# Loads behind marker stores in the start-up of a decay-attention and softplus-FFN kernel

## The chip, the core and the metric

The kernel runs on one core of a Trainium2 chip. A core has a matrix engine (TensorE, PE in the profile; its weight loads are PEld), a vector engine (VectorE, DVE), a scalar engine (ScalarE, ACT), a general engine (GpSimd, POOL) and a synchronising engine (SyncE, SP) that here issues nearly all DMA transfers. Each engine has its own instruction stream and runs it in order; semaphores tie the streams together. The metric is device time in microseconds of one execution, lower is better.

## The reference

Attention with a decaying state, for 4 batches, 8 heads, 768 positions and 64 dimensions, in blocks of 64 positions, and then a feed-forward layer on the 3072 tokens of 512 values:

```python
for b in range(nb):                       # 12 blocks of 64 positions
    intra = np.einsum('bhic,bhjc->bhij', qb, kb) * Dmask[None]
    intra = np.einsum('bhij,bhjd->bhid', intra, vb)
    inter = np.einsum('bhid,bhde->bhie', qb * lam_pow[None], kv_state)
    out[:, :, sl] = intra + inter
    kb_dec = kb * rev_pow[None]
    kv_state = lam_block[None, :, None, None] * kv_state + np.einsum('bhsd,bhse->bhde', kb_dec, vb)
...
h = x @ w_in                              # 512 -> 2048
g = np.maximum(h, 0.0) + np.log1p(np.exp(-np.abs(h)))
return (g @ w_out).astype(np.float32)     # 2048 -> 512
```

`q`, `k`, `v` and the decay `lam` are float32; the two weight matrices are float64 as drawn.

## The kernel before

The 768 positions are cut into six chunks of 128 (two blocks each). The attention of one chunk and one pair of heads is a *unit*: 24 units in all, four per chunk. Unit `g` is loaded by `load_upto` (L84) in two DMA transfers of 512 KB. The weights come in 32 *banks* of 512 KB, half of them of the first matrix, half of the second, loaded by `w_load` (L126) as raw 64-bit words into tiles `raw`. A bank is converted on the chip: `w_scale` and `w_round` on ScalarE (L213, L217), `w_shift`, `w_sign` and `w_add` on VectorE (L221, L225, L231), then split into a high and a low part, `w_hi` on ScalarE (L234) and `w_lo` on VectorE (L238). Both layers' matmuls run as three products of such parts.

A unit has these steps. `k_decay` (L281 for unit 0, L285 otherwise, on ScalarE) and `q_decay` (L292) scale keys and queries. `mm_scores` (L307, L309; `xy` in the order list) forms scores and state updates on TensorE; in the first chunk one matmul at L301 opens it. `mask_scores` (L334) multiplies by the decay mask; `first_states` (L347) and `next_states` (L359) copy states on ScalarE, `carry_states` (L354) carries them on TensorE. `mm_out` (L322, L326; `z`) forms the unit's output, and `x_high` (L371, ScalarE) and `x_low` (L378, VectorE) split it into parts for the feed-forward layer.

The feed-forward layer runs in 96 *slots*: 6 chunks times 16 slices of 128 of the 2048 hidden values. `mlp1` (L406) makes a slot's hidden values from four units' outputs, `chain_act` (L387, softplus), `chain_hi` (L391) and `chain_lo` (L395) make its parts `g`, and `mlp2` (L423) adds them into four output banks, one per batch. At a chunk's last slot each bank is copied out by ScalarE or VectorE (L429) and stored (L431).

Eight DMA semaphores are used in turn, so SP issues a transfer only when the one eight places earlier has landed. Work goes to the engines in the order in which the code is written: a list of named steps for the first chunk's attention and the first slots (`for line in """ ... """`), and a loop over slots after it. In the list, `load n` loads weight banks up to n, `unit n` units up to n, and `warm n` issues n filler matmuls (L146) into a bank that nobody reads. `act`, `ghi` and `glo` are a slot's `chain_*` steps. Ahead of the list, units 0 to 3 and weight banks are loaded in turn, 18 fillers run, and the decay tables are built.

Of the kernel before, what the change touches and what calls it, by code (L numbers as in the profile page):

```python
# [7 lines left out]
F32 = mybir.dt.float32  # L8
# [6 lines left out]
B, H, S, D = 4, 8, 768, 64  # L15
C = 128
T = 64
NCH = S // C
NP = H // 2
# [7 lines left out]
def half(i):  # L27
    return slice(i * 64, (i + 1) * 64)
# [3 lines left out]
def decay_attention_softplus_ffn(  # L32
# [7 lines left out]
    nc = tc.nc  # L40
    ctx.enter_context(tc.manual_schedule())
    cp = ctx.enter_context(tc.tile_pool(name="cp", bufs=1))
# [5 lines left out]
    def t8(shape, dt, name):  # L48
        return sb.tile(shape, dt, tag="b8", bufs=21, name=name)
# [4 lines left out]
    def t2(shape, dt, name):  # L54
        return sb.tile(shape, dt, tag="b2", bufs=5, name=name)
# [7 lines left out]
    def obank(name):  # L63
        return ps.tile([128, 512], F32, tag="o", bufs=4, name=name)
# [5 lines left out]
    def bank(name):  # L70
        return ps.tile([128, 512], F32, tag="h", bufs=2, name=name)
# [8 lines left out]
    def load_upto(n):  # L80
        for g in range(len(units), min(n, NG)):
            t = t8([128, 2, 2, 512], F32, f"att{g}")
            for major in range(2):
                nc.sync.dma_start(out=t[:, major], in_=att[g // NP, g % NP, :, major])  # L84
            units.append(t)
# [33 lines left out]
    def w_load(n):  # L119
        nonlocal n_raw  # L120
        while n_raw < min(n, NW):
            k = n_raw
            if k % 2 == 0:
                raws[k] = raws[k + 1] = t8([128, 2, DM, 2], U32, f"raw{k}")
            f, which = w_order[k]
            nc.sync.dma_start(  # L126
                out=raws[k][:, k % 2].rearrange("q n t -> q (n t)"), in_=wts[f, which].bitcast(U32)
            )
            n_raw += 1

    for n in range(NP - 1):
        load_upto(n + 1)
        w_load(n + 1)
    load_upto(NP)
    w_load(7)
    load_upto(NP + 1)


    spare = t8([128, 4, 512], F32, "spare")
    warm = t8([128, 512], F32R, "warm")  # L140
# [12 lines left out]
    for s in range(2):  # L153
# [7 lines left out]
        out=begins[0], in_=ramp.rearrange("q (o i) -> q o i", o=1).broadcast_to([128, H, T]), scalar=0.0,  # L161
# [9 lines left out]
    def powers(out, n):  # L171
# [19 lines left out]
        out=diag[half(1)], in0=off[half(1)].rearrange("q (o i) -> q o i", o=1).broadcast_to([64, H, T]), scalar=0.0,  # L191
# [48 lines left out]
    def w_of(f, which):  # L240
        j, i = divmod(w_order.index((f, which)), 2)
        return w_pairs[j][:, :, i]
# [7 lines left out]
    def x_of(c, p):  # L250
        if (c, p // 2) not in x_tiles:
            x_tiles[c, p // 2] = t8([128, 2, 2, 512], F32R, f"x_{c}_{p // 2}")
        return x_tiles[c, p // 2][:, :, p % 2]

    aa, kds, qds, states = {}, {}, {}, {}
    lo, hi = half(0), half(1)
# [5 lines left out]
    def first_chunk(g):  # L262
        return g < NP
# [6 lines left out]
    def own(g, n, name):  # L270
        if not first_chunk(g):
            return t2([128, B, 2, 64], F32, f"{name}_{g}")
        if g not in spares:
            spares[g] = t8([128, 3, B, 2, 64], F32, f"own_{g}")
        return spares[g][:, n]
# [107 lines left out]
    h_tiles, l_tiles, g_tiles, o_tiles = {}, {}, {}, {}  # L383
# [13 lines left out]
    def mlp1(s, ps_=range(NP)):  # L397
        c, f = divmod(s, NF)
        if s not in h_tiles:
            h_tiles[s] = bank(f"h{s}")  # L400
        w = w_of(f, 0)
        for p in ps_:
            cs = slice(p * 128, (p + 1) * 128)
            x = x_of(c, p)
            for n, (i, j) in enumerate(((0, 0), (1, 0), (0, 1))):
                nc.tensor.matmul(  # L406
                    h_tiles[s], lhsT=w[:, i, cs], rhs=x[:, j, :],
                    start=p == 0 and n == 0, stop=p == NP - 1 and n == 2,
                )

    def mlp2(ss):
        c = ss[0] // NF
        ends = ss[-1] % NF == NF - 1
        if ss[0] % NF == 0:
            o_tiles[c] = [obank(f"o{c}_{b}") for b in range(B)]
        if ends:
            ob = t8([128, B, 512], F32, f"ob{c}")
        for b in range(B):
            for s in ss:
                f = s % NF  # L420
                g, w = g_tiles[s], w_of(f, 1)
                for n, (i, j) in enumerate(((0, 0), (0, 1), (1, 0))):
                    nc.tensor.matmul(  # L423
                        o_tiles[c][b], lhsT=g[:, i, b * 128 : (b + 1) * 128], rhs=w[:, j],
                        start=f == 0 and n == 0, stop=f == NF - 1 and n == 2,
                    )
            if ends:
                copy = nc.vector.tensor_copy if b % 2 else nc.scalar.copy
                copy(out=ob[:, b], in_=o_tiles[c][b])  # L429
                queue = nc.scalar if c == NCH - 1 and b % 2 == 0 else nc.sync  # L430
                queue.dma_start(out=out[b * S + c * C : b * S + (c + 1) * C, :], in_=ob[:, b])  # L431
# [11 lines left out]
    xy, z = {}, {}  # L443
# [5 lines left out]
    def end(p):  # L449
# [6 lines left out]
        "dg": lambda p: carry_states(p, xy[p][1]), "sl": lambda p: next_states(p, xy[p][1]), "xh": lambda p: x_high(p, z[p]),  # L456
        "xl": lambda p: x_low(p, z[p]), "scale": w_scale, "round": w_round, "shift": w_shift, "sign": w_sign,
        "add": w_add, "hi": w_hi, "lo": w_lo, "act": chain_act, "ghi": chain_hi, "glo": chain_lo,
        "mlp": lambda s, *ps_: mlp1(s, ps_ or range(NP)), "scores": scores_of, "load": w_load, "unit": load_upto, "warm": keep_warm,
    }  # L460
    for line in """
        q 0, k 0, xy 0, scale 0, round 0, a 0, st 0, q 1, warm 3, shift 0, sign 0, z 0, add 0, k 1, xh 0,
        xl 0, hi 0, xy 1, dg 0, scale 1, lo 0, st 1, a 1, q 2, round 1, mlp 0 0, warm 4, sl 0, shift 1,
        sign 1, z 1, add 1, k 2, xy 2, dg 1, xh 1, xl 1, hi 1, scale 2, round 2, lo 1, a 2, st 2, sl 1, q
        3, mlp 0 1, warm 4, load 8, shift 2, sign 2, add 2, k 3, z 2, xy 3, xh 2, xl 2, hi 2, scale 3,
        round 3, shift 3, a 3, st 3, lo 2, sign 3, dg 2, mlp 0 2, warm 2, add 3, z 3, mlp 1 0, mlp 1 1,
        mlp 1 2, scale 4, round 4, xh 3, hi 3, sl 2, xl 3, shift 4, lo 3, sign 4, add 4, load 10, mlp 0 3,
        mlp 1 3, scale 5, round 5, q 4, k 4, act 0, ghi 0, hi 4, shift 5, sign 5, add 5, lo 4, dg 3, mlp
        2, act 1, ghi 1, hi 5, glo 0, glo 1, lo 5, scale 6 7, round 6 7, scores 4, unit 6, load 12, act 2,
        ghi 2, mlp 3, glo 2, sl 3, shift 6 7, sign 6 7, add 6 7  # L470
    """.replace("\n", " ").split(","):
        name, *numbers = line.split()
        step[name](*map(int, numbers))
# [11 lines left out]
    for s in range(LAG, last + LAG):  # L485
# [19 lines left out]
        if s == last + LAG - 2:  # L505
            mlp2([s - LAG, s - LAG + 1])
        elif s - LAG < last - 1 and s - 1 not in both_at:
            mlp2([s - LAG])
# [4 lines left out]
        if s in both_at:  # L513

            g = both_at[s]
            w, x, y = work(f"z{g - 1}"), bank(f"x{g}"), bank(f"y{g}")
            mm_out(g - 1, w)
            mm_scores(g, x, y)
            mask_scores(g, x)
            x_high(g - 1, w)  # L520
            update_states(g, y)
            x_low(g - 1, w)
            if g < NG - 1:
                keep_values(g)
            mlp2([s + 1 - LAG])
# [51 lines left out]
```

## Time and profile before

| | |
|---|---|
| Time, three runs | 607.14, 607.69 (median), 608.19 us |
| The profiled execution | 607.95 us |
| Its span, first to last instruction of the program | 606.2 us |
| TensorE busy | 596.9 us, 98% of the span |
| VectorE, ScalarE busy | 226.4 us, 219.8 us |
| HBM read, written | 41.95 MB, 6.29 MB |

The span is shorter than the time by 1.75 us, which lies outside the program's instructions. A matmul's end is modelled, and matmuls overlap, so a busy TensorE is not one at its peak. In a row of a timeline stand the start, the length in us, the engine, the line of the code, the operation, the tiles written and read, their shapes and the number of instructions merged; in brackets stands the idle time of the engine before it and what ended it. "issue" there means that nothing which the profile records ended the wait. In rows of grouped waits stand the total in us, how often, and the longest. A row of stretches has the stretch, its length, for each engine the busy time and the number of instructions, then TensorE's granted clock (1.00 is full), the mean busy share of the 16 DMA engines, and GB/s.

### The profile page before, as it was taken

How to read it: one execution, taken by the hardware profiler on the slowest of the kernel's cores; microseconds unless marked ns; L12 is line 12 of the kernel's file. 1: busy time of each engine (PE TensorE's matmuls, PEld its weight loads, DVE VectorE, ACT ScalarE, POOL GpSimd, SP SyncE). 2: the span in 40 equal slices, each digit the busy share in tenths (PEclk: the TensorE clock that was granted, in tenths of full speed). 3: DMA queues.
4: the chain of work that ended last, by engine and by line, in shares of the span. 5: the costliest groups of instructions: out<-in, count | busy, mean ns of one | idle time of the engine just before them, and what ended most of it. 6: DMA issues, size and time to landing. Idle time of an engine off the chain costs nothing.

```text
span 606.2 us, 11776 instructions
## 1 busy us (share of the span) xinstructions
PE 596.9 (98%) x5299; PEld 488.5 (81%) x5299; DVE 226.4 (37%) x336; ACT 219.8 (36%) x355; POOL 4.7 (1%) x11
## 2 busy tenths in 40 slices
PE   9899999999999999999999999999999999999997
PEld 6577888888888888888888888888888888888886
DVE  7779999853232233132222321321312211211111
ACT  3777777633222223332223323222333121322121
POOL 3000000000000000000000000000000000000000
PEclk9999999999999999999999999999999999999999
DMA  8995314216002023300120500211500000100001
GB/s 297 406 406 227 122 74 141 88 52 208 3 2 70 1 70 98 112 2 11 61 70 29 182 2 0 71 32 40 207 3 1 1 1 1 69 2 0 1 0 69
DMA packets 15169, 48.98 MB, mean 81 GB/s; under 512 B 1808, under 2 KB 1808, under 8 KB 15120
## 3 DMA queue, kind: packets, MB, share of 16 engines
q1 hardware_dynamic: 14832, 47.72, 21.8%
q8 instruction: 41, 0.67, 0.4%
q10 hardware_dynamic: 288, 0.52, 0.2%
q14 instruction: 8, 0.07, 0.0%
HBM read 41.95 MB, written 6.29 MB: 80 GB/s over the span
## 4 chain that ended last, share of the span: by engine, by line
PE 91%; DMA 7%; DVE 1%; SPq 1%; ACT 0%; issue 0%
PE o L423 43%; PE h L406 41%; DMA raw<-in_wts 5%; PE z L322 2%; PE x L307 2%; DMA att<-in_att 2%; PE z L326 2%; PE w L307 1%; PE y L309 1%; SPq L84 0%; DVE w L238 0%; DVE c L231 0%; DVE c L225 0%; SPq L126 0%; ACT w L234 0%; PE w L309 0%
## 5 line engine op out<-in xcount | busy, mean ns | idle before, releaser
L423 PE MATMUL o<-w,g 128*128 128x512 f32 x1152 | 278.9, 391 | 1.1 <-DVE w L238 0.8
L406 PE MATMUL h<-x,w 128*128 128x512 f32 x1152 | 276.8, 391 | 0.0
L423 PEld LDWEIGHTS o<-w,g 128*128 128x128 f32 x1152 | 215.0, 188 | 47.2 <-DVE w L238 1.1
L406 PEld LDWEIGHTS h<-x,w 128*128 128x128 f32 x1152 | 215.1, 188 | 46.7 <-issue 1.2
L395 DVE TENSOR_TENSOR g<-l,g 128x512 fp32r<-128x512 f32 x96 | 66.4, 692 | 310.4 <-ACT g L391 310.2
L387 ACT ACTIVATE l<-h 128x512 f32<-128x512 f32 x96 | 57.4, 598 | 309.0 <-PE h L406 306.4
L391 ACT CAST g<-l 128x512 fp32r<-128x512 f32 x96 | 59.6, 621 | 3.1
L371 ACT CAST x<-z 128x512 fp32r<-128x512 f32 x24 | 14.0, 585 | 41.4 <-PE z L326 41.4
L334 DVE TENSOR_TENSOR a<-x,mask 128x512 f32<-128x512 f32 x15 | 10.4, 692 | 36.1 <-PE y L309 26.4
L339 DVE SCALAR_TENSOR_TENSOR st<-st,lam_c,y 64x256 f32<-64x256 f32 x52 | 22.9, 480 | 0.8
L322 PEld LDWEIGHTS z<-qd,st 64*64 64x64 f32 x640 | 17.0, 134 | 7.0 <-issue 7.0
L307 PE MATMUL x<-att 64*64 64x64 f32 x608 | 21.9, 219 | 0.0
L213 ACT ACTIVATE c<-raw 128x1024 f32<-128x1024 f32 (+1 forms) x19 | 19.0, 1001 | 7.3 <-DMA raw<-in_wts 7.3
L234 ACT CAST w<-c 128x1024 fp32r<-128x1024 f32 (+1 forms) x19 | 17.4, 914 | 10.3 <-DVE c L231 7.7
L238 DVE TENSOR_TENSOR w<-c,w 128x1024 fp32r<-128x1024 f32 (+1 forms) x19 | 20.0, 1053 | 2.8 <-ACT w L234 2.7
L231 DVE CUSTOM_DVE_ANT_0 c<-raw,c 128x2048 uint16<-128x2048 uint16 (+1 forms) x19 | 20.1, 1058 | 2.4
L322 PE MATMUL z<-qd,st 64*64 64x64 f32 x640 | 20.9, 224 | 0.0
L307 PEld LDWEIGHTS x<-att 64*64 64x64 f32 x608 | 20.0, 135 | 1.0 <-PE z L326 0.5
L225 DVE SCALAR_TENSOR_TENSOR c<-raw,c 128x1024 uint32<-128x1024 uint32 (+1 forms) x19 | 20.1, 1056 | 0.6
L378 DVE TENSOR_TENSOR x<-z,x 128x512 fp32r<-128x512 f32 x24 | 16.6, 690 | 7.9 <-ACT x L371 7.5
L217 ACT ACTIVATE raw<-raw 128x1024 uint32<-128x1024 uint32 (+1 forms) x19 | 18.9, 993 | 0.0
L285 ACT ACTIVATE kd<-att,rp 128x256 f32<-128x256 f32 x40 | 18.1, 502 | 0.0
(54 smaller groups left out, 230.5 us busy)
## 6 DMA issues: line engine op xcount, KB each, us to landing
att<-in_att SPq DMA_DIRECT2D x48, 512.0 KB, 5.5
raw<-in_wts SPq DMA_DIRECT2D x32, 512.0 KB, 10.2
out_dram<-ob SPq DMA_DIRECT2D x22, 256.0 KB, 2.2
out_dram<-ob ACTq DMA_DIRECT2D x2, 256.0 KB, 2.0
lam_b<-in_lam SPq DMA_DIRECT2D x1, 4.0 KB, 2.6
```

Source lines behind the costliest of these rows:

```text
L213: nc.scalar.activation(c.bitcast(F32), raw_at(ks, 1).bitcast(F32), AF.Copy, scale=2.0**-112)
L225: nc.vector.scalar_tensor_tensor(out=c, in0=raw_at(ks, 1), scalar=0x80000000, in1=c, op0=ALU.bitwise_and, op1=ALU.bitwise_or)
L231: nc.vector.tensor_add(out=c, in0=c, in1=raw_at(ks, 0))
L238: nc.vector.tensor_sub(out=w[:, 1], in0=conv.pop(ks[0]).bitcast(F32), in1=w[:, 0])
L307: nc.tensor.matmul(x[r, cols], lhsT=k[r, b, t], rhs=q[r, b, t], start=True, stop=True)
L322: nc.tensor.matmul(w[half(t), s, cols], lhsT=st[r, b, t], rhs=qd[r, b, t], start=True, stop=False)
L339: nc.vector.scalar_tensor_tensor(out=to[:, :, t], in0=of[:, :, t], scalar=lam_c[r, h : h + 1], in1=u[:, :, t], op0=ALU.mult, op1=ALU.add,)
L387: nc.scalar.activation(l_tiles[s], h_tiles.pop(s), AF.Softplus)
L391: nc.scalar.copy(out=g_tiles[s][:, 0, :], in_=l_tiles[s])
L395: nc.vector.tensor_sub(out=g[:, 1, :], in0=l_tiles.pop(s), in1=g[:, 0, :])
L406: nc.tensor.matmul(h_tiles[s], lhsT=w[:, i, cs], rhs=x[:, j, :], start=p == 0 and n == 0, stop=p == NP - 1 and n == 2,)
L423: nc.tensor.matmul(o_tiles[c][b], lhsT=g[:, i, b * 128 : (b + 1) * 128], rhs=w[:, j], start=f == 0 and n == 0, stop=f == NF - 1 and n == 2,)
```

## The change

Four things change. Loads: unit 3 is issued right after unit 2, weight bank 2 after it, and every later load of the first chunk stands behind a *marker*, a DMA store of four values from a tile that ScalarE writes into a small tile `marks`. SP issues in order, so it waits there until ScalarE has written that tile. `fk p` marks unit p's decayed keys, `fs p` its states, `fg s` the high part of slot s. Unit 4 comes ahead of weight banks 6 and later. Fillers: the last two groups, of 4 and 2, are dropped. ScalarE: slot 0's softplus and cast stand ahead of unit 4's decayed keys. End: the last output bank is copied in halves of 256 columns, the first by ScalarE and the second by VectorE, each stored by SP.

```diff
-    for n in range(NP - 1):
+    for n in range(2):
         load_upto(n + 1)
         w_load(n + 1)
     load_upto(NP)
-    w_load(7)
-    load_upto(NP + 1)
+    w_load(3)
+
+
+    marks = cp.tile([128, 32], F32, name="marks")
+    n_marks = 0
+
+    def fence(ap):
+        nonlocal n_marks
+        nc.sync.dma_start(out=marks[64:65, 4 * n_marks : 4 * n_marks + 4], in_=ap)
+        n_marks += 1
...
-            if ends:
+            if ends and c == NCH - 1 and b == B - 1:
+
+                for n, copy in enumerate((nc.scalar.copy, nc.vector.tensor_copy)):
+                    cols = slice(n * 256, (n + 1) * 256)
+                    copy(out=ob[:, b, cols], in_=o_tiles[c][b][:, cols])
+                    nc.sync.dma_start(out=out[b * S + c * C : b * S + (c + 1) * C, cols], in_=ob[:, b, cols])
+            elif ends:
...
+        "fk": lambda p: fence(own(p, 0, "kd")[64:65, 0, 0, 0:4]), "fs": lambda p: fence(states[p][64:65, 0, 0, 0:4]),
+        "fg": lambda s: fence(g_tiles[s][64:65, 0, 0:4].bitcast(F32)), "warm": keep_warm,
...
-        3, mlp 0 1, warm 4, load 8, shift 2, sign 2, add 2, k 3, z 2, xy 3, xh 2, xl 2, hi 2, scale 3,
...
-        round 3, shift 3, a 3, st 3, lo 2, sign 3, dg 2, mlp 0 2, warm 2, add 3, z 3, mlp 1 0, mlp 1 1,
...
+        sign 1, z 1, add 1, k 2, fk 2, load 5, xy 2, dg 1, xh 1, xl 1, hi 1, scale 2, round 2, lo 1, a 2,
+        st 2, fs 2, load 6, sl 1, q 3, mlp 0 1, shift 2, sign 2, add 2, k 3, fk 3, unit 5, z 2, xy 3, xh
+        2, xl 2, hi 2, scale 3, round 3, shift 3, a 3, st 3, fs 3, load 8, lo 2, sign 3, dg 2, mlp 0 2,
...
```

What SP issues from the unit-2 load on. Before (`att` are units, `raw` pairs of weight banks; a row with x2 is a whole unit or two banks):

```order
L84 DMA att_78<-in_att 128x1024 x2
L126 DMA raw_81<-in_wts 128x1024
L84 DMA att_83<-in_att 128x1024 x2
L126 DMA raw_81<-in_wts 128x1024
L126 DMA raw_87<-in_wts 128x1024 x2
L126 DMA raw_90<-in_wts 128x1024
L84 DMA att_92<-in_att 128x1024 x2
L126 DMA raw_90<-in_wts 128x1024
L126 DMA raw_494<-in_wts 128x1024 x2
L84 DMA att_587<-in_att 128x1024 x2
```

And with the change, where a row with `marks` is a marker:

```order
L84 DMA att_78<-in_att 128x1024 x2
L84 DMA att_81<-in_att 128x1024 x2
L126 DMA raw_84<-in_wts 128x1024
L143 DMA marks<-own_253 1x4x1
L126 DMA raw_84<-in_wts 128x1024
L126 DMA raw_297<-in_wts 128x1024
L143 DMA marks<-st_344 1x4x1
L126 DMA raw_297<-in_wts 128x1024
L143 DMA marks<-own_349 1x4x1
L84 DMA att_360<-in_att 128x1024 x2
L143 DMA marks<-st_433 1x4x1
L126 DMA raw_436<-in_wts 128x1024 x2
```

Unit 3 (second row) has moved ahead of weight bank 2, which is now the eleventh transfer of 512 KB instead of the ninth; bank 3 and all after it stand behind a marker. Three more markers follow, on the high parts of slots 0, 1 and 2, ahead of banks 8, unit 5 with banks 9 and 10, and bank 11.

What TensorE does between unit 2's scores and its output, before:

```order
L309 MATMUL y_304<-att_78,own_261 64x64
L354 MATMUL y_219<-st_258,spare 64x4x64 x2
L406 MATMUL h_264<-x_0_213,w_216 128x512 x3
L146 MATMUL warm_ps<-warm 128x512 x4
L322 MATMUL z_366<-own_261,st_348 64x64 x2
L326 MATMUL z_366<-own_261,att_78 64x64 x4
```

With the change:

```order
L317 MATMUL y_300<-att_78,own_253 64x64
L362 MATMUL y_211<-st_250,spare 64x4x64 x2
L414 MATMUL h_256<-x_0_205,w_208 128x512 x3
L330 MATMUL z_363<-own_253,st_344 64x64 x2
L334 MATMUL z_363<-own_253,att_78 64x64 x4
```

The four fillers are gone (lines have shifted by 8); one unit later two more are gone in the same place.

What ScalarE does around slot 0's softplus, before (`kd` is unit 4's decayed keys):

```order
L213 ACTIVATE c_503<-raw_87 128x512
L217 ACTIVATE raw_87<-raw_87 128x512
L285 ACTIVATE kd_508<-att_92,rp_126 128x4x64 x2
L387 ACTIVATE l_511<-h_264 128x512
L391 CAST g_513<-l_511 128x512
L234 CAST w_515<-c_483 128x512
L387 ACTIVATE l_536<-h_473 128x512
```

With the change:

```order
L221 ACTIVATE c_499<-raw_297 128x512
L395 ACTIVATE l_501<-h_256 128x512
L225 ACTIVATE raw_297<-raw_297 128x512
L399 CAST g_504<-l_501 128x512
L242 CAST w_509<-c_482 128x512
L293 ACTIVATE kd_517<-att_360,rp_118 128x4x64 x2
L395 ACTIVATE l_535<-h_472 128x512
```

Slot 0's softplus has moved ahead of the rounding of bank 5, and unit 4's keys behind the high part of bank 4; slot 1's softplus still follows them all.

More of the change, by code (lines that the diff above doesn't have):

```diff
@@ L458, in decay_attention_softplus_ffn @@
         "add": w_add, "hi": w_hi, "lo": w_lo, "act": chain_act, "ghi": chain_hi, "glo": chain_lo,
-        "mlp": lambda s, *ps_: mlp1(s, ps_ or range(NP)), "scores": scores_of, "load": w_load, "unit": load_upto, "warm": keep_warm,
+        "mlp": lambda s, *ps_: mlp1(s, ps_ or range(NP)), "scores": scores_of, "load": w_load, "unit": load_upto,
+        "fk": lambda p: fence(own(p, 0, "kd")[64:65, 0, 0, 0:4]), "fs": lambda p: fence(states[p][64:65, 0, 0, 0:4]),
+        "fg": lambda s: fence(g_tiles[s][64:65, 0, 0:4].bitcast(F32)), "warm": keep_warm,
     }
@@ L463, in decay_attention_softplus_ffn @@
         xl 0, hi 0, xy 1, dg 0, scale 1, lo 0, st 1, a 1, q 2, round 1, mlp 0 0, warm 4, sl 0, shift 1,
-        sign 1, z 1, add 1, k 2, xy 2, dg 1, xh 1, xl 1, hi 1, scale 2, round 2, lo 1, a 2, st 2, sl 1, q
-        3, mlp 0 1, warm 4, load 8, shift 2, sign 2, add 2, k 3, z 2, xy 3, xh 2, xl 2, hi 2, scale 3,
-        round 3, shift 3, a 3, st 3, lo 2, sign 3, dg 2, mlp 0 2, warm 2, add 3, z 3, mlp 1 0, mlp 1 1,
[L467 to L470, printed above, removed]
+        sign 1, z 1, add 1, k 2, fk 2, load 5, xy 2, dg 1, xh 1, xl 1, hi 1, scale 2, round 2, lo 1, a 2,
+        st 2, fs 2, load 6, sl 1, q 3, mlp 0 1, shift 2, sign 2, add 2, k 3, fk 3, unit 5, z 2, xy 3, xh
+        2, xl 2, hi 2, scale 3, round 3, shift 3, a 3, st 3, fs 3, load 8, lo 2, sign 3, dg 2, mlp 0 2,
+        add 3, z 3, mlp 1 0, mlp 1 1, mlp 1 2, scale 4, round 4, xh 3, hi 3, sl 2, xl 3, shift 4, lo 3,
+        sign 4, add 4, mlp 0 3, mlp 1 3, scale 5, act 0, round 5, ghi 0, fg 0, load 9, hi 4, shift 5, sign
+        5, add 5, lo 4, q 4, k 4, dg 3, mlp 2, act 1, ghi 1, fg 1, unit 6, load 11, hi 5, glo 0, glo 1, lo
+        5, scale 6 7, round 6 7, scores 4, act 2, ghi 2, fg 2, load 12, mlp 3, glo 2, sl 3, shift 6 7,
+        sign 6 7, add 6 7
     """.replace("\n", " ").split(","):
```

## The prediction

> **What bounds the kernel now.** I read the page's engines and queues first, then what TensorE (PE) waited for over the whole span.
>
> ```profile
> PE 596.9 (98%) x5299; PEld 488.5 (81%) x5299; DVE 226.4 (37%) x336; ACT 219.8 (36%) x355; POOL 4.7 (1%) x11
> ...
> q8 instruction: 41, 0.67, 0.4%
> ```
>
> ```profile
> PE z L326 <- issue: 2.4, 2, 1.4
> ...
> PE o L423 <- DVE w L238: 0.8, 1, 0.8
> PE z L322 <- issue: 0.6, 1, 0.6
> ...
> ```
>
> PE is busy 98% of the span, so time can come only from its idle stretches, its filler matmuls (L146), or from before and after it. These rows hold most of its idle time behind the first matmul. Three waits (2.4 and 0.6) are put down to "issue": nothing that the profile shows ended them. Next, the last of them on PE's timeline, and how many matmuls PE had started just before the ends of the second and third (24.2, 30.7) and at certain other moments (columns: stretch, length, PE busy and count, clock, DMA share, GB/s).
>
> ```profile
> 30.71 0.36 PE L326 MATMUL z<-own,att 64*64 64x64 f32 x9 [1.44 <-issue]
> ...
> 0.00:21.67 21.67, 19.25 (x329) 1.00 0.90 330
> 0.00:24.20 24.20, 21.26 (x348) 1.00 0.91 337
> 0.00:28.10 28.10, 25.13 (x454) 1.00 0.93 347
> 0.00:30.70 30.70, 26.29 (x475) 1.00 0.94 352
> 0.00:543.08 543.08, 537.55 (x5038) 1.00 0.25 88
> ```
>
> From stall to stall are 127 matmuls, each with a weight load: 254 instructions and a semaphore or two. The page's instruction queue q8 moved 0.67 MB in 41 packets, 16 KB each, for 2 x 5299 instructions of PE: some 258 per packet. So PE stops where its next block of code is missing. The DMA view of 0.2 us around 21.7, 28.1 and 543.1 has one such packet each:
>
> ```profile
> q8 instruction: 1, 0.02, 32.0%
> ...
> q8 instruction: 1, 0.02, 32.1%
> ...
> q8 instruction: 1, 0.02, 33.5%
> ```
>
> In the start-up these packets begin 348 - 329 = 19 and 475 - 454 = 21 matmuls before the block is needed, and PE goes on 2.5 to 2.6 us after their start (21.67 to 24.2, 28.10 to 30.71). Late in the run, 37 packets x 256 = 9472 instructions after the third stall less 2 x (5038 - 475) = 9126 leaves the block at 543.1 some 150 to 170 matmuls ahead (an estimate; semaphores count too). What differs is the DMA load:
>
> ```profile
> 20.00:30.00 10.00, 8.71 (x188) 5.93 (x179) 7.70 (x13) 7.40 (x14) 0.00 (x0) 1.00 1.03 407
> 60.00:70.00 10.00, 10.00 (x97) 8.34 (x90) 9.71 (x14) 7.89 (x11) 0.00 (x0) 1.00 0.30 102
> ```
>
> At 407 GB/s a 0.524 MB load takes 1.29 us, and SP keeps eight queued. The Trainium skill ("Runtime: NRT & Kernel Launch", Instruction fetch mechanics) also has 16 KiB blocks of 256 instructions, but calls their cost mostly hidden; here three are not.
>
> **The loads behind markers.** To landing, the loads issued at 9.3 (eleventh) and 72.0 took:
>
> ```profile
> L84 SPq DMA_DIRECT2D att<-in_att x1: 328/328/328, 9.3 to 9.3; - x1
> DMA to landing us min/median/max: 11.7/11.7/11.7
> ...
> L126 SPq DMA_DIRECT2D raw<-in_wts x1: 328/328/328, 72.0 to 72.0; - x1
> DMA to landing us min/median/max: 3.4/3.4/3.4
> ```
>
> With the change SP stops after its eleventh load, issued at 9.3 as now, until unit 2's decayed keys are written:
>
> ```profile
> 16.75 0.91 ACT L285 ACTIVATE own<-att,rp 128x256 f32<-128x256 f32 x2
> ```
>
> That load ends the queue at 9.3 + 11.7 = 21.0; two more behind the marker end it by 23.6. A code packet cannot wait for more than what is queued: the second packet starts by 21.0 at the latest (PE on by 23.6), the third by 23.6 (on by 26.2). The first stall (2.4 - 1.44 = 1.0) has the queue of before up to 9.3, and stays.
>
> PE, ACT and DVE rows around the two stalls:
>
> ```profile
> 22.09 1.09 PE L146 MATMUL warm_ps<-warm 128*128 128x512 f32 x4
> 23.12 0.27 PE L322 MATMUL z<-own,st 64*64 64x64 f32 x2
> 25.01 0.45 PE L301 MATMUL y<-warm 64*64 64x512 f32 x1
> 28.70 0.27 PE L322 MATMUL z<-own,st 64*64 64x64 f32 x2
> 31.44 3.70 PE L406 MATMUL h<-x,w 128*128 128x512 f32 x15
> ```
>
> ```profile
> 20.08 0.69 ACT L213 ACTIVATE c<-raw 128x512 f32<-128x512 f32 x1
> 21.36 0.58 ACT L347 COPY st<-y 64x512 f32<-64x512 f32 x1
> 22.45 0.91 ACT L285 ACTIVATE own<-att,rp 128x256 f32<-128x256 f32 x2
> 25.12 0.59 ACT L371 CAST x<-z 128x512 fp32r<-128x512 f32 x1 [1.76 <-PE z L326]
> 27.39 0.58 ACT L347 COPY st<-y 64x512 f32<-64x512 f32 x1
> ...
> 29.19 0.69 DVE L231 CUSTOM_DVE_ANT_0 c<-raw,c 128x1024 uint16<-128x1024 uint16 x1
> 32.18 0.69 DVE L378 TENSOR_TENSOR x<-z,x 128x512 fp32r<-128x512 f32 x1 [2.29 <-ACT x L371]
> ```
>
> Weight bank 2 was the ninth load and is now the eleventh, two loads later: its scaling on ACT moves from 20.08 to 21.0, and behind it on ACT stand round, unit 2's states (L347), the keys of unit 3 (L285). L347 ends 21.0 + (21.94 - 20.08) = 22.9, so z 2 on PE starts at 22.9 and not 23.12: of the four fillers removed ahead of it (1.03 us from 22.09) only 0.2 is saved. z took 25.01 - 23.12 = 1.89 with a stall of 0.6, so 1.3 without; z 2 ends by 24.2. The block's end then falls in z 2 after 18 matmuls instead of 14, at about 23.4, so the second packet, at its bound, is late by 0.2; I take it as in time, since no packet so far started behind all that was queued.
>
> ACT: L285 ends at 23.36 + 0.9 = 24.3, the cast of z 2 follows there (25.12 now), so its stretch to unit 3's states ends at 27.97 - 0.85 = 27.1. PE: from L301 to z 3 now 28.70 - 25.01 = 3.69, less two fillers (0.55): 3.14, so z 3 starts at 24.2 + 3.14 = 27.3. Its block ends 25 matmuls in, near 27.9; the third packet was on by 26.2. So no third stall, and z 3 ends 27.3 + 1.3 = 28.6 against 31.44: **2.8 saved**. With z at the 1.1 that remains if a restart costs 0.2 it is 3.2. DVE's next x (L378, 32.18) could start behind L231 at 29.88 - 0.85 = 29.0 and behind the cast at about 29.2: about 3.0. I take 3.0.
>
> **Whether it lasts.** Up to 50.2 ACT and DVE set PE's pace in places:
>
> ```profile
> 38.14 0.69 DVE L395 TENSOR_TENSOR g<-l,g 128x512 fp32r<-128x512 f32 x1
> 38.94 0.60 ACT L387 ACTIVATE l<-h 128x512 f32<-128x512 f32 x1 [2.20 <-DVE g L395]
> 48.76 1.13 ACT L213 ACTIVATE c<-raw 128x1024 f32<-128x1024 f32 x1
> 50.17 2.79 PE L423 MATMUL o<-w,g 128*128 128x512 f32 x11 [0.77 <-DVE w L238]
> ```
>
> DVE runs eleven instructions without a gap from L378 at 32.18 to L395 at 38.14, and frees the buffer for the second activation; that chain reaches L238, and PE at 50.17. It has the same instructions after the change and starts 3.0 earlier, so PE's wait of 0.8 there stays and everything moves by 3.0. Slot 0's activation ahead of unit 4's keys (0.91) hides behind ACT's 2.20 wait: both stand before it; without that cover it would cost 0.9 at most. Removing fillers costs no clock in the sum: 1.00 is granted through stalls up to 1.4, and the change leaves none longer.
>
> The fenced loads must not be late. Weight 9 waits for the marker of slot 1, whose cast ends some 0.65 behind L387's 39.54 (a cast of this size, L371, takes 0.59): 40.2, then 37.2; unit 5's two loads stand ahead of it. Issued from 37.5 they land at 37.5 + 3.4 = 40.9 and 42.2, and it at 43.5; scaling needs them at 48.76 - 3.0 = 45.8: 2.3 to spare. Weights 6 and 7, behind unit 3's states at 27.1, land by 32.3; their scaling follows that cast on ACT, after 37. The seven markers cost SP about 0.33 each of a queue that waits anyway; four values each, no engine waits for them.
>
> **The last bank.** Rows of the end (the last store took 2.0 to land):
>
> ```profile
> 602.49 0.69 DVE L429 COPY ob<-o 128x512 f32<-128x512 f32 x1 [2.03 <-PE o L423]
> 603.21 0.33 SPq L431 DMA_DIRECT2D out_dram<-ob  x1
> DMA to landing us min/median/max: 2.0/2.0/2.0
> ```
>
> Half a bank on ACT and half on DVE: between half of 0.59 to 0.69 and, by L285's 0.50 per 256 columns, 0.5: stores issue near 602.95 and 603.3. The second is 0.1 later than the one now; half the bytes at 407 GB/s save 0.32 of its landing or nothing. -0.2 to +0.1; I take -0.05.
>
> **Sum.** The profiled execution took 607.95; less 3.0 and 0.05: 604.9. The median shown, 607.69, lies 0.26 lower: **604.6**.
>
> **Rivals.** *The packets start as late as now* (0.11). By 24.23 and 30.71 PE could not go on; z 3 would have 23 matmuls left instead of 29 and end 0.2 earlier: 607.4. For it: no row has a packet behind a queue of two or three loads. Against it: 19 and 21 matmuls ahead under 407 GB/s, 150 and more later. The Trainium skill speaks for it ("DMA: Bandwidth & Descriptors", Queues, rings and completion order): each DMA engine takes turns between the queues it has work for, a packet at a time, so a code packet would wait for one packet, however long the load queue. The 19 and 21 against 150 do not agree; by the rule the time is 607.4.
>
> *One of the two stalls stays* (0.12), the second: its packet's bound, 23.6, already lies past the 23.4 at which PE wants it. If it comes as late as now, PE goes on at 24.2 and z 2 ends about 25.1 instead of 24.2, with ACT and DVE behind it: 0.9 to 1.1 given back, 605.6.
>
> *PE's wait for L238 goes too* (0.05): slot 0's earlier activation could shorten the chain into it; 0.8 more, 603.8. Against it: that chain starts at DVE's 38.14, not at the activation.
>
> *The fenced loads are late* (0.06), the slower side. Place: weight 9 behind slot 1's marker and unit 5. It decides once it lands after 45.8; a loss needs 2.3 + 3.0 = 5.3 us more than reckoned, as when the loads behind a marker took the 11.7 of a full queue instead of 3.4: 43.5 + 8.3 = 51.8, 6.0 late, and 604.6 + 6.0 = 610.6 with none of it hidden. Against it: the 3.4 at 72.0 followed a pause just like these.
>
> **Numbers.** The forecast has 0.66. Its own range is 603.9 to 605.4 (2.8 to 3.2, tail, half of ACT's reorder). The range for 8 in 10 takes in the case with one stall and touches the better one: 603.4 to 606.3. About 0.2% (1.2 us) is what a measurement here can tell from none: faster 0.66 + 0.12 + 0.05 = 0.83, same 0.11, slower 0.06.
>
> **What would show it.** Right: PE's "issue" waits fall from 3.0 to about 1.0, the second packet starts before 21, z 3's L406 starts near 28.6, the wait on L238 stays near 0.8 and comes near 47. Wrong: a wait for raw weights on ACT after 40, packets still about 20 matmuls ahead, or a wait of PE on ACT between 30 and 45 that has no row now.

## The result and the profile after

The change takes **604.44 us** (median of four, 603.79 to 604.52) against 607.67 for the kernel before on the same chip (607.14 to 608.19): a ratio of 0.9943, 95% interval 0.9930 to 0.9955; the medians differ by 3.2 us. Times here and below are medians without four executions that count as slow, 846.84 (the profiled one) and 3389.53 us of the kernel with the old order on ScalarE, 618.78 and 618.80 us of the one with four queued, bank 2 first and four fillers out. The profiled execution took 604.39, its span is 602.6 (606.2 before). Its page, engines and the queue of code packets:

```profile
PE 595.4 (99%) x5293; PEld 487.4 (81%) x5293; DVE 226.6 (38%) x336; ACT 220.4 (37%) x356; POOL 4.1 (1%) x11
...
q8 instruction: 41, 0.67, 0.5%
```

What TensorE waited for behind its start, largest waits first (engine, line, what ended the wait; total us, how often, longest):

```profile
PE o L431 <- DVE w L246: 0.8, 1, 0.8
PE z L334 <- issue: 0.7, 1, 0.7
PE o L431 <- ACT w L242: 0.4, 1, 0.4
PE z L330 <- ACT st L355: 0.2, 1, 0.2
```

Of three waits put down to "issue" (2.4 and 0.6 in all) one is left, of 0.7. The packets of q8 in the trace's records begin at these moments, in us from the start of the span:

| | first | second | third | fourth | fifth |
|---|---|---|---|---|---|
| before | 15.58 | 21.67 | 28.10 | 34.44 | 43.23 |
| after | 15.48 | 19.19 | 23.56 | 29.48 | 37.03 |

The rows of TensorE's timeline that answer to those of the prediction:

```profile
17.98 0.21 PE L334 MATMUL z<-own,att 64*64 64x64 f32 x1 [0.74 <-issue]
...
22.37 0.27 PE L330 MATMUL z<-own,st 64*64 64x64 f32 x2 [0.25 <-ACT st L355]
...
23.45 0.45 PE L309 MATMUL y<-warm 64*64 64x512 f32 x1
...
26.68 0.27 PE L330 MATMUL z<-own,st 64*64 64x64 f32 x2
...
27.75 3.69 PE L414 MATMUL h<-x,w 128*128 128x512 f32 x15
...
46.53 0.74 PE L431 MATMUL o<-w,g 128*128 128x512 f32 x2 [0.76 <-DVE w L246]
```

The work behind z 3 (L414) starts at 27.75 instead of 31.44: 3.69 gained by there. At the wait for bank 4's last step the gain is 50.17 - 46.53 = 3.64, at the end of TensorE's work 602.45 - 599.12 = 3.33; from there to the end of the span 3.48 instead of 3.71. The granted clock is 1.00 from the start of its records at 7.60 to the end of TensorE's work.

ScalarE, in the start-up and at the first step of weight banks 8 and 9:

```profile
20.48 0.68 ACT L221 ACTIVATE c<-raw 128x512 f32<-128x512 f32 x1 [0.43 <-DMA raw<-in_wts]
...
21.74 0.58 ACT L355 COPY st<-y 64x512 f32<-64x512 f32 x1
...
45.39 1.14 ACT L221 ACTIVATE c<-raw 128x1024 f32<-128x1024 f32 x1 [0.17 <-DMA raw<-in_wts]
```

Bank 2 came at 20.45, ahead of the 21.0 foreseen, and held ScalarE by 0.43. The last row was not foreseen: bank 9, the second of a pair that is scaled together, arrived just after it was needed and not 2.3 us ahead. The stretches of that time (columns as before: the stretch, its length, engines, clock, DMA share, GB/s) show how slowly the loads moved:

```profile
37.00:38.00 1.00, 1.00 (x6) 0.82 (x5) 1.00 (x3) 1.00 (x2) 0.00 (x0) 1.00 0.11 25
38.00:39.00 1.00, 1.00 (x6) 0.84 (x5) 0.98 (x3) 1.00 (x2) 0.00 (x0) 1.00 0.73 217
39.00:40.00 1.00, 1.00 (x6) 0.81 (x6) 0.97 (x3) 0.97 (x3) 0.00 (x0) 1.00 0.88 315
...
43.00:44.00 1.00, 1.00 (x6) 0.84 (x5) 1.00 (x1) 0.00 (x0) 0.00 (x0) 1.00 0.94 352
44.00:45.00 1.00, 0.88 (x4) 0.38 (x2) 0.74 (x2) 0.83 (x1) 0.00 (x0) 1.00 1.03 410
```

The first load behind the pause was issued at 37.37 and landed at 40.68; the second, issued at 37.75, landed at 44.02. From 38 to 44 the loads run at 217 to 356 GB/s, and at 410 only after that. That so few are queued explains it at most at first: by the trace's issues and landings seven loads are on their way from 43.3 to 44, and the stretch from 43 to 44 still shows 352. What holds the rate down until 44 is open.

### The profile page after: what moved, and what is told of

It is laid out like the page before. It is cut to its first block, busy times and chain, and to the rows that moved or that the text cites. A ratio compares the mean times of both kernels' runs of the same rounds, so it can differ in the third digit from the quotient of the medians.

```text
span 602.6 us, 11785 instructions
## 1 busy us (share of the span) xinstructions
PE 595.4 (99%) x5293; PEld 487.4 (81%) x5293; DVE 226.6 (38%) x336; ACT 220.4 (37%) x356; POOL 4.1 (1%) x11
## 4 chain that ended last, share of the span: by engine, by line
PE 93%; DMA 3%; DVE 1%; ACT 1%; issue 0%; SPq 0%; ACTq 0%; DVEq 0%
PE o L431 44%; PE h L414 42%; DMA raw<-in_wts 3%; PE z L330 2%; PE x L315 2%; PE z L334 2%; PE y L317 1%; PE w L315 1%; DVE c L233 0%; DVE c L239 0%; DVE w L246 0%; ACT l L395 0%; ACT w L242 0%; ACT raw L225 0%; DVE c L229 0%
## 5 line engine op out<-in xcount | busy, mean ns | idle before, releaser
L414 PE MATMUL h<-x,w 128*128 128x512 f32 x1152 | 276.7, 391 | 0.0
L414 PEld LDWEIGHTS h<-x,w 128*128 128x128 f32 x1152 | 215.1, 188 | 46.5 <-ACT c L221 0.8
L347 DVE SCALAR_TENSOR_TENSOR st<-st,lam_c,y 64x256 f32<-64x256 f32 x52 | 22.9, 480 | 0.8
```

What stands on the lines that cost most here:

```text
L347: nc.vector.scalar_tensor_tensor(out=to[:, :, t], in0=of[:, :, t], scalar=lam_c[r, h : h + 1], in1=u[:, :, t], op0=ALU.mult, op1=ALU.add,)
L414: nc.tensor.matmul(h_tiles[s], lhsT=w[:, i, cs], rhs=x[:, j, :], start=p == 0 and n == 0, stop=p == NP - 1 and n == 2,)
```

## The experiments

The theory: a code packet for TensorE waits behind the data loads that are queued, so fewer queued loads bring it forward. The first rival: the loads don't matter, and the gain comes from the removed fillers, from ScalarE's order or from the tail. In the table, "stalls" are TensorE's waits put down to "issue", and "packets" the moments at which the first three code packets begin, both from the profiled execution, of which the kernel with the old order on ScalarE has none here; ratios are against the kernel before, run beside each.

| kernel | time, us | ratio, 95% | packets | stalls |
|---|---|---|---|---|
| before | 607.67 | | 15.58, 21.67, 28.10 | 0.93, 0.55, 1.44 |
| the change | 604.44 | 0.9930 to 0.9955 | 15.48, 19.19, 23.56 | 0.74 |
| loads and markers alone | 605.18 | 0.9953 to 0.9976 | 15.47, 19.85, 23.34 | 0.74 |
| change without markers | 608.43 | 1.0005 to 1.0028 | 15.66, 21.83, 28.28 | 1.04, 1.01 |
| same, six fillers back | 607.57 | 0.9994 to 1.0012 | 15.53, 21.66, 28.03 | 0.76, 0.56, 1.43 |
| before, six fillers out | 607.80 | 0.9997 to 1.0017 | 15.20, 21.48, 27.81 | 0.5, 1.48 |
| before, last bank in halves | 607.64 | 0.9991 to 1.0008 | 15.37, 21.42, 27.78 | 0.43, 0.56, 1.43 |
| change, old order on ScalarE | 604.48 | 0.9938 to 0.9964 | | |
| change, bank 2 first | 604.10 | 0.9931 to 0.9957 | 15.38, 18.91, 22.87 | 0.47 |
| four queued, markers on weights too | 611.78 | 1.0054 to 1.0126 | 18.99, 22.42, 30.04 | none |
| same, bank 2 first, four fillers out | 613.51 | 1.0055 to 1.0126 | 19.31, 22.90, 32.87 | none |
| four queued, markers on units | 612.15 | 1.0053 to 1.0100 | 13.95, 19.87, 27.29 | none |
| same, bank 2 first | 606.10 | 0.9960 to 0.9983 | 14.07, 18.42, 24.58 | none |
| five queued, markers on units, bank 2 first | 604.89 | 0.9940 to 0.9967 | 13.53, 18.76, 22.57 | none |

### The loads alone, and the markers

The first kernel has the change's load order and markers, with fillers, ScalarE's order and the last bank as before:

```
-        ..., mlp 0 1, shift 2, ...        dg 2, mlp 0 2, add 3, ...
+        ..., mlp 0 1, warm 4, shift 2, ...   dg 2, mlp 0 2, warm 2, add 3, ...
-        scale 5, act 0, round 5, ghi 0, fg 0, load 9, hi 4, ... lo 4, q 4, k 4, dg 3,
+        scale 5, round 5, q 4, k 4, act 0, ghi 0, fg 0, load 9, hi 4, ... lo 4, dg 3,
```

> The loads' new order and the markers alone: the six fillers, ScalarE's order and the whole last bank are as before. Theory (late code packets under a full load queue): the second and third "issue" waits of TensorE (0.6 and 1.4) go, the fillers' time stays; z 3 ends near 29.1 instead of 31.4, so about 2.3 less than before: 605.4. Rival (the dropped fillers and the order carry the gain, packets are not held by the queue): no more than 0.3 less, 607.4.

605.18. The last two stalls are gone with the fillers still there, so the loads do it; by the medians 2.5 of the 3.2 us come from them alone. TensorE's waits have one "issue" row:

```profile
PE z L334 <- issue: 0.7, 1, 0.7
```

The second kernel is the change with the marker stores left out and all else kept, so that SP queues loads as deep as before:

```
     def fence(ap):
-        nonlocal n_marks
-        nc.sync.dma_start(out=marks[64:65, 4 * n_marks : 4 * n_marks + 4], in_=ap)
-        n_marks += 1
+        return
```

> The changed kernel with no marker stores, all else kept: SP runs ahead again until eight loads are queued. Theory: code packets start about as late as before (near 21.7 and 28), PE waits longer at both places since the fillers no longer fill them, and all but 0.2 to 0.5 of the gain is lost: 607.1 to 607.5. Rival (the fillers and the order carry the gain): 604.5 to 604.9, no wait above 0.3 at those places.

608.43: the gain is gone, and the packets begin when they did before the change. That settles it against the rival. It is also 0.9 us above the upper end of what the theory said. Two stalls of 1.0 were left, and behind them the clock fell; here are TensorE's waits and two stretches:

```profile
PE z L333 <- issue: 2.0, 2, 1.0
```

```profile
21.91:25.32 3.41, 2.00 (x52) 1.25 (x50) 2.34 (x4) 2.29 (x6) 0.00 (x0) 1.00 1.01 404
25.32:28.70 3.38, 3.38 (x69) 2.46 (x68) 2.26 (x4) 3.20 (x6) 0.00 (x0) 0.50 1.04 411
```

The granted clock is 0.50 from 25.32 for 10.24 us. This execution took 610.12; the twelve run from 607.17 to 610.91. The three of them with a mean clock of 1.00 took 607.21 to 607.64, as long as the kernel before: the gain is lost without the fall too.

### The fillers and the clock

The kernel before, without the six fillers that the change removes:

```
-        3, mlp 0 1, warm 4, load 8, ...   dg 2, mlp 0 2, warm 2, add 3, ...
+        3, mlp 0 1, load 8, ...           dg 2, mlp 0 2, add 3, ...
```

> The kernel before without the last two groups of fillers (4 and 2), nothing else. Theory: their 1.6 us turns into longer "issue" waits, since the packets pin the second and third restart: 607.5, at most 0.3 less than before. Rival (fillers were plain cost on TensorE): 1.6 less, 606.1. A third way: the granted clock falls without them and the time rises.

607.80, no difference that can be measured; but the third way shows, as the clock is 0.50 from 25.24 for 6.83 us in the profiled execution (608.48), right behind a stretch of 3.41 us that holds the stall of 1.48. To see whether the absent fillers made the kernel without markers slow, they were put back into it:

```
 (the change without its marker stores)
-        ..., mlp 0 1, shift 2, ...        dg 2, mlp 0 2, add 3, ...
+        ..., mlp 0 1, warm 4, shift 2, ...   dg 2, mlp 0 2, warm 2, add 3, ...
```

> The change without its marker stores, as in the earlier run that took 608.43 with two stalls of 1.0 and a granted clock of 0.5 for 10.24 us, but with the six filler matmuls of units 1 and 2 put back. Theory (without the fillers, stalls of this length let the clock fall, and that made the earlier run slower than the kernel before): two or three stalls as in the kernel before, the clock at 1.00 from its first rise to the end of PE's work, 607.2 to 607.7. Rival (the clock falls by the stalls alone, or what was slow was the order of the loads): clock 0.5 for 3.4 us or more, 608 or above.

607.57, back to the time of before. By the medians the fillers are worth 0.9 us here, where the stalls stay, but the two intervals overlap (1.0005 to 1.0028 without them, 0.9994 to 1.0012 with them), so no gain in time is shown. Eight of its executions lie between 607.21 and 607.76 and three near 609.1, and the profiled one is of these; here are the window of its third stall and the next:

```profile
28.46:31.87 3.41, 1.98 (x51) 1.57 (x51) 1.18 (x2) 1.11 (x3) 0.00 (x0) 1.00 1.02 404
31.87:35.28 3.41, 3.41 (x9) 2.62 (x8) 3.19 (x6) 1.73 (x4) 0.00 (x0) 0.50 1.03 408
```

The other executions have a mean clock each, and 3.41 us at one half takes 0.003 off it. It is 0.997 or less in 9 of 12 executions without markers and fillers and in 10 of 12 of the kernel before without fillers, but in 3 of 11 with the fillers back and in 13 of the 65 of the kernel before that ran beside the experiments. So the fillers make the fall rarer, not impossible: neither theory holds as it was put. In its profiled execution the kernel before has the same in the window of its own third stall, with a clock that stays:

```profile
27.78:31.19 3.41, 1.97 (x49) 1.38 (x49) 1.97 (x4) 1.45 (x3) 0.00 (x0) 1.00 1.01 400
```

1.97 and 1.98 busy of 3.41, the one kept, the other not. What decides between them isn't settled by these runs. That the change can drop the fillers fits its having removed the stalls that they stood against: its mean clock is 0.999 or 1.00 in all four executions, and its 604.44 is 0.7 below the 605.18 with fillers, which has the old order on ScalarE and the old tail besides. The change with nothing but the fillers put back was not run.

### ScalarE's order, the tail, bank 2

Unit 4's keys put back ahead of slot 0's softplus, in the change:

```
-        scale 5, act 0, round 5, ghi 0, fg 0, load 9, hi 4, ... lo 4, q 4, k 4, dg 3,
+        scale 5, round 5, q 4, k 4, act 0, ghi 0, fg 0, load 9, hi 4, ... lo 4, dg 3,
```

> The changed kernel with unit 4's decayed keys again ahead of slot 0's softplus on ScalarE. Theory: both stand ahead of slot 1's softplus, ahead of which ScalarE idles 1.48, so the order is worth nothing: 604.4, within 0.3. Rival: the keys' 0.9 reaches TensorE: 605.3.

604.48; its interval overlaps the change's: no difference that these runs can tell. The kernel before with the last bank copied and stored in halves, and nothing else:

```
-            if ends:
+            if ends and c == NCH - 1 and b == B - 1:
+                for n, copy in enumerate((nc.scalar.copy, nc.vector.tensor_copy)):
+                    ...
+            elif ends:
```

> The kernel before with the last output bank copied and stored in halves, nothing else. By the changed kernel's end (TensorE's last matmul to the end of the span 3.48 instead of 3.71) 0.25 less: 607.4. Rival (the two stores share SP and cost what the halves save): no difference, 607.7.

607.64, a ratio of 0.9999: not to be told from nothing. From TensorE's end to the span's end it is 3.55 instead of 3.71. The copies don't run side by side, as two rows of its timeline show:

```profile
602.18 0.37 ACT L431 COPY ob<-o 128x256 f32<-128x256 f32 x1 [0.77 <-PE o L423]
...
602.59 0.42 DVE L431 COPY ob<-o 128x256 f32<-128x256 f32 x1 [2.43 <-ACT ob L431]
```

VectorE's half waits for ScalarE's, though they write and read different columns. The Trainium skill ("PSUM — Partial Sum Buffer", PSUM bank collisions raise a hardware error) says that accesses of two engines to one bank have to be ordered by bank and quarter of the partitions, not by address; the wait agrees with a program that orders them so, and no run here shows what happens without it.

Bank 2 put back ahead of unit 3 in the change, with its markers:

```
-    for n in range(2):
+    for n in range(3):
         load_upto(n + 1)
         w_load(n + 1)
     load_upto(NP)
-    w_load(3)
```

> The changed kernel with weight bank 2 issued ahead of unit 3, as before the change; markers kept. Theory: its landing (the eleventh place, near 20.45) held ScalarE by 0.43 and TensorE's z 2 by 0.25; in the ninth place it lands near 18, both waits go: 0.2 to 0.4 less than the changed kernel, 604.1. Rival: unit 3's keys, now waiting for the eleventh place, take the same time back: 604.4.

604.10, as the theory had it, and no difference from the change by the intervals. z 2 no longer waits for bank 2 and starts at 21.87; but a new wait stands in the list, and its span is the change's, 602.6:

```profile
PE w L314 <- DVE x L385: 0.6, 1, 0.6
PE z L333 <- issue: 0.5, 1, 0.5
```

### Pacing the first loads too

The change leaves the first stall, because its markers begin behind the eleventh load. If the depth of the queue is the cause, pacing those eleven brings the first packet forward too. The first try kept four loads queued, by a marker store that reads what the load four places earlier has brought:

```
+    for n, what in enumerate("u00 u01 w0 u10 u11 w1 u20 u21 u30 u31 w2".split()):
+        if n >= 4:
+            fence(landed[n - 4])    # four values of the unit half or raw bank
+        ...                         # then this load
```

> The changed kernel with the first eleven loads paced too: from the fifth on each load stands behind a marker that reads the load four places earlier, so four are queued and not eight, at the same rate. Theory (the depth of the load queue holds code packets): the first packet starts at least 1 earlier than 15.5 and the first "issue" wait (0.7) goes; the time hardly moves, 604.0 to 604.5, since ScalarE then waits for bank 2 near 20.5. Rival (the rate, not the depth, holds them): packet near 15.5, wait 0.7, 604.4. A third way: pacing starves the loads and bank 2 comes later: 605 or more.

611.78, and the packet was later, at 18.99. The experiment had a flaw of its own. Rows of ScalarE and of TensorE:

```profile
14.04 0.65 ACT L235 ACTIVATE raw<-raw 128x512 uint32<-128x512 uint32 x1 [4.08 <-DMA marks<-raw]
```

```profile
15.44 0.37 PE L340 MATMUL z<-own,st 64*64 64x64 f32 x2 [3.98 <-ACT st L365]
```

ScalarE's rounding overwrites a raw bank in place, so it has to wait until the marker store that reads the bank has landed, and that store stands behind the loads queued ahead of it. TensorE stopped for 4 us, and the clock fell for 10.24 us. With bank 2 first and the four fillers ahead of unit 1's output out it was the same, with a wait of 4.33 and 17.07 us at half clock:

> As the run paced at four, with bank 2 ahead of unit 3 and the fillers ahead of unit 1's output (4) dropped as well. Theory: with the first packet in time z 1 starts about 1.0 earlier and does not stop, 1.7 in all, of which ScalarE's keys and the loads let through 1.0 to 1.6: 602.9 to 603.5. Rival: the granted clock falls to 0.5 for some microseconds, as in the runs that dropped fillers and kept the late packets: 605 or more, and widely spread.

613.51. Both miss their theory; 605 or more stands among the rivals, but none names ScalarE's wait for the marker, which came ahead of the rest. They say nothing on the packet, since TensorE itself was late. The next two pace by markers that read unit tiles alone, which nothing overwrites:

```
-            fence(landed[n - 4])
+            past = first[n - 4] if first[n - 4][0] == "u" else first[n - 3]
+            fence(units[int(past[1])][64:65, int(past[2]), 0, 0:4])
```

> The pacing of the two runs before stalled ScalarE for 4 us: its rounding overwrites a raw weight bank in place, and the marker store that read two words of that bank landed only behind the loads queued ahead of it. Here the first eleven loads are paced to about four in the queue again, in the order of the change, but the markers read unit tiles alone, which nothing overwrites. Theory (a code packet waits for what is queued ahead of it): no wait for a marker, the first packet starts before 14.6 instead of 15.48, and the first stall falls from 0.74 to under 0.4; but bank 2 is the eleventh load and lands near 22.1 as in the paced run, 1.7 us later than with the change, so that z 2 waits up to 1.5 us for it: 604.6 to 605.9. Rival (the packet's time is not set by the queue's depth): the stall stays at 0.7 and bank 2's lateness comes on top: 605.3 to 606.3.

> As the run with markers on unit tiles, and bank 2 ahead of unit 3. Theory: first packet before 14.6, first stall under 0.4, bank 2 in time; unit 3 lands near 22 instead of 19.2, so its keys start up to 1 us late and z 3 may wait for them: 603.9 to 604.7, and below 604.0 only if z 3 doesn't wait. Rival (depth isn't it): stall 0.7, 604.5 to 605.4.

Both have no "issue" wait at all, with first packets at 13.95 and 14.07: the theory's part on the packet holds. The count of matmuls that TensorE had started says it best: 177 and 185 when the packets began. The change had started as many by 13.55 and 13.67, and its packet began at 15.48, 1.9 and 1.8 us later. z 1 in the second of them runs without a break:

```profile
17.14 0.27 PE L338 MATMUL z<-own,st 64*64 64x64 f32 x2
17.15 0.27 PE L342 MATMUL z<-own,att 64*64 64x64 f32 x2
17.24 0.23 PE L338 MATMUL z<-own,st 64*64 64x64 f32 x2
17.26 0.33 PE L342 MATMUL z<-own,att 64*64 64x64 f32 x8
```

The times are 612.15 and 606.10, far over what was expected of the first and over both the theory's 603.9 to 604.7 and the rival's 605.4 for the second; the profiled executions, 609.58 and 604.90, are among the fastest of their kernels. Four queued loads don't keep the rate: in the stretch from 10 to 12 the DMA engines moved 236 GB/s in the second, 418 with the change.

```profile
10.00:12.00 2.00, 2.00 (x75) 1.51 (x68) 1.34 (x2) 1.17 (x3) 1.28 (x1) 1.00 0.66 236
```

```profile
10.00:12.00 2.00, 2.00 (x75) 1.52 (x69) 1.33 (x2) 1.21 (x3) 1.28 (x1) 1.00 1.02 418
```

So units 1 to 3 come late, ScalarE waits for them (1.24, 1.29 and 0.52 us), and TensorE starts 74 matmuls from 12 to 14 where the change starts 96. With bank 2 last ScalarE waits longer, and these are its waits in that kernel; 7.3 of the first row is the wait for the first bank at 9.3, as long in the other kernels, and 3.0 the one for bank 2:

```profile
ACT c L229 <- DMA raw<-in_wts: 10.3, 2, 7.3
ACT own L301 <- DMA att<-in_att: 3.6, 2, 2.4
```

There TensorE stood 1.1 and 0.8 us, and the clock was 0.50 from 20.35 for 10.24 us. The last run takes five queued and bank 2 first:

```
-        if n >= 4:
-            past = first[n - 4] if first[n - 4][0] == "u" else first[n - 3]
+        if n >= 5:
+            past = first[n - 5] if first[n - 5][0] == "u" else first[n - 4]
```

> As the run with the first eleven loads paced to four and bank 2 ahead of unit 3, which had no stall for code left (first packet at 14.07) but got unit 1 at 12.5 instead of 11.85 and units 2 and 3 late too, so that TensorE waited for their decayed keys; here five are queued. Theory (the depth of the queue sets the packet's time, and four was too few to keep the loads at their rate): unit 1 lands by 12.0 and its keys are in time, the first packet starts between 14.2 and 14.9, the first stall is under 0.2, and the time is 603.4 to 604.1, at or below the 604.10 of the run with bank 2 first and no pacing. Rival (whatever brings the packet forward costs the same in late units): 604.3 to 605.5. Third way (five queued hold the packet as eight do): first packet at 15.2 or later, stall 0.5, 603.9 to 604.4.

Here both halves of the theory hold in the start-up: the loads keep 416 GB/s from 10 to 12, the first packet is at 13.53, ahead of the 14.2 to 14.9 expected and when TensorE had started 182 matmuls, no stall is left, units are in time, and z 3 ends at 26.9, 0.95 ahead of the change. Around that packet the loads moved less, though: 352 GB/s from 13 to 14, against 406 with the change, and behind it, here and then with the change:

```profile
14.00:16.00 2.00, 2.00 (x8) 1.12 (x7) 1.89 (x4) 1.95 (x4) 0.00 (x0) 1.00 0.91 303
```

```profile
14.00:16.00 2.00, 2.00 (x15) 1.18 (x8) 1.89 (x4) 1.95 (x4) 0.00 (x0) 1.00 1.04 410
```

So a shallower queue and a lower rate go together at that moment, and no run here holds one and varies the other. And yet the kernel takes 604.89 (604.12 to 605.20), which lies in the rival's range, with a span of 602.5: only 0.1 of the 0.95 is left in the span, and nothing in the time. ScalarE, VectorE and TensorE of that kernel, at 45 and at 56 us:

```profile
45.40 1.13 ACT L229 ACTIVATE c<-raw 128x1024 f32<-128x1024 f32 x1 [1.13 <-DMA raw<-in_wts]
```

```profile
55.37 0.68 DVE L394 TENSOR_TENSOR x<-z,x 128x512 fp32r<-128x512 f32 x1
...
56.11 0.27 PE L323 MATMUL w<-att 64*64 64x64 f32 x1 [0.94 <-DVE x L394]
```

and the same places with the change (PEld is TensorE's weight load):

```profile
55.36 0.68 DVE L386 TENSOR_TENSOR x<-z,x 128x512 fp32r<-128x512 f32 x1
...
56.10 0.13 PEld L315 LDWEIGHTS w<-att 64*64 64x64 f32 x1 [0.44 <-DVE x L386]
```

In both kernels banks 8 and 9 reach ScalarE at 45.4 (that row of the change stands above), though one issued bank 9's load 1.1 us earlier (why it lands no sooner is open), and in both the row of VectorE to which TensorE's wait ahead of unit 4's scores is put down ends near 56.05. From 45.4 to 59, ScalarE's and VectorE's rows agree to 0.02 us. So, as long as these banks land when they do, the change has used up what could be gained at the start: TensorE now comes to unit 4's scores just as VectorE lets it, and what is gained ahead of that is given back as a wait there (0.94, and 0.55 in the run with bank 2 first). The way from the landing to VectorE's row is read from the order of the rows; a kernel with those banks loaded earlier was not run.

## Why the prediction was right

The forecast, 604.6 against 604.44, went by the mechanism that the runs show, and its two large rivals fell. Point by point:

**The code packets.** "PE stops where its next block of code is missing", and the packet comes later behind eight queued loads than behind few: shown by the kernel with loads and markers alone, by the one without markers, and by the first packet's 13.5 to 14.1 with four or five loads queued against 15.5 with eight, while TensorE's own rows up to there lie at the same places within about 0.4 us. The sign that the prediction named for being wrong, packets still about 20 matmuls ahead, is not there: the second and third begin when TensorE has started 259 and 379, some 90 and 95 short of the block ends at 348 and 475 that the prediction read off the kernel before. These runs don't tell the depth of the queue from the rate of the loads as what delays a packet. The rival by the Trainium skill ("DMA: Bandwidth & Descriptors", Queues, rings and completion order), that a packet of another queue waits for one packet of the loads however many there are, doesn't agree with that: at the same count of matmuls the first packet began 1.8 to 1.9 us later with eight queued than with four or five. The measurement decides.

**The size of the gain.** Taken was 3.0 between 2.8 and 3.2; it was 3.69 at z 3's end. The start of z 2 was reckoned 22.9 and is 22.37, since bank 2 landed at 20.45 and not 21.0. z 2 took 23.45 - 22.37 = 1.08, near the 1.1 that the prediction named and did not take, and not 1.3. These two terms were mis-sized by 0.5 and by 0.2 for each of two z.

**"Everything moves by 3.0".** The wait for bank 4's last step stayed (0.76), as forecast, and the gain there was 3.64. But of the 3.69 only 3.33 reached the end of TensorE's work: 0.09 went before unit 4's scores, where VectorE is the new bound, and 0.2 more by the end, without a wait of its own that would show where. With the tail the profiled executions differ by 607.95 - 604.39 = 3.56, against 3.05 in the sum; two errors of opposite sign, 0.7 gained more and 0.35 given back, and the tail are behind that. The median of before lies 0.26 below its profiled execution and that of the change 0.05 above, which takes back 0.3. That the forecast came within 0.2 is luck; the steps were off by more.

**The fenced loads.** The margin of 2.3 us was wrong: the step "land at 37.5 + 3.4 = 40.9 and 42.2, and it at 43.5" held for the first load (40.68), while the next came 3.3 later (44.02) and bank 9 at about 45.4, as ScalarE's wait for it shows, and scaling began at 45.39 with no margin left. The 3.4 at 72.0 was one load behind a pause; for several the rate matters, and it was 217 to 356 GB/s and not the 407 of the full queue. Each marker took SP 0.60 to 0.73 and not 0.33. The wait for raw weights on ScalarE after 40, named as a sign of being wrong, is there with 0.17. The slower rival was nearer than the margin of 2.3 says, and the run with five queued met its mechanism as a wait of 1.13.

**"Removing fillers costs no clock."** Right for the change, and its reason, a clock of 1.00 through stalls up to 1.4, wrong: behind stalls of 1.0 to 1.5 the clock fell to 0.50 in two kernels without the fillers, and now and then with them.

**The tail.** Reckoned -0.05 with the halves side by side; they run one after the other, yet each store of 128 KB lands 1.73 after its issue instead of 2.0 for 256 KB. From TensorE's end to the span's end the change is 0.23 shorter, the halves alone 0.16, which no time could tell from nothing.

**ScalarE's order.** Costed at nothing, and the run that undoes it can't be told from the change.

## What to carry to other kernels

Where a profile shows waits that nothing ends, at a constant number of instructions apart, look for the code packets and at what else is queued for DMA: here a new order of the loads and a shallower queue of them were worth 2.5 us with not an instruction of arithmetic changed. The depth has two sides, as four queued loads gave up the rate (236 against 418 GB/s) and eight held the code back, so it has to be tried; and a marker is a reader of what it marks, so let it read only what nothing will overwrite soon. A gain at the start is worth what the next bound leaves of it: before making more of it, look how far behind the other engines are where they meet again.

## What was not expected of the hardware

In the profiled executions of three kernels the granted clock fell to one half right behind a stretch with no wait longer than 1.5 us, in which TensorE was busy for 1.94 to 2.00 of 3.41 us, mostly with matmuls of 64x64. Over all six kernels in whose profile it fell before TensorE's end it stayed there for 3.41, 6.83, 10.24 (three of them) or 17.07 us: one, two, three or five times 3.41. The Trainium skill ("TensorE: Matmul & The Clock Gate", Part 1, What's actually happening) has a free-running window of 3413 ns; the lengths agree. Its table of what matters for a kernel ("Why this matters for your kernels") asks only that no idle gap be longer than about 3 us; here windows whose longest wait was 1.0 to 1.5 went ahead of the fall, and the kernel before had as much idle time in such a window of its profiled execution and kept its clock.

Loads behind a pause ran at 217 to 356 GB/s for some 6 us, in the last of these with seven on their way, against 400 and more in the full queue of the start-up.
